# Summing k' over the tiles by accumulating DMAs, and another order of the part products

## The chip, the core and the metric

The kernel runs on one core of one Trainium2 chip. The metric is the time of one execution on the device in microseconds, as the median of a few runs. The profile is one execution of the same program, recorded by the hardware profiler.

## The reference

The inputs are x (2048 rows, D = 576 columns), a weight for q, k and v, an output weight, the two real DFT matrices over the sequence (2048 x 2048) and the two over D (576 x 576), and a gate vector. Cut to what matters:

```python
qkv = x @ wqkv                                  # q, k, v of 32 heads with 18 columns
phi = lambda t: where(t > 0, t + 1, exp(t)) + 1e-6
pq, pk = phi(q), phi(k)
kv  = einsum("bhsd,bhse->bhde", pk, v)
z   = einsum("bhsd->bhd", pk)                   # the sum of k' over the sequence
num = einsum("bhqd,bhde->bhqe", pq, kv)
den = einsum("bhqd,bhd->bhq", pq, z)[..., None] + 1e-6
a   = (num / den) @ wo
b   = dft_seq_re @ (x @ dft_hid_re.T) - dft_seq_im @ (x @ dft_hid_im.T)
g   = sigmoid((x * gate_w).sum(-1))
out = g * a + (1 - g) * b
```

## The kernel before

Every f32 product is made of three TensorE products of rounded parts: each operand is split into a high part (a ScalarE copy that rounds, `hi_of`, L167) and a low part (a VectorE subtraction, `lo_of`, L177), and high x high, high x low and low x high are added up in one PSUM bank. Nearly every matmul has 128 rows, 128 stationary columns and 288 moving columns, half of D.

The stages follow one another on TensorE:

- k' (L512 for the first four tiles of 128 rows of x, then L197): 16 tiles. `feature` makes k' from PSUM with two ScalarE operations and one VectorE operation (L336) and leaves it in `acc[i]`, an SBUF tile of 128 x 576 f32. `k_split` makes its two parts (`pk[i]`).
- k'^T x (L637): 20 steps, four for each of five column blocks c of x; a step takes four tiles. The x tiles `c` come by `xg_load` and are split by `xg_next` two steps ahead of their use. After the second step of each c, `kv_step` (L619, L622) multiplies by wv.
- In the same steps k' is summed over the 16 tiles for z. VectorE adds one `acc` tile to `zacc` in each step (`add`, L187). At step 15 `z_chain` adds the 16 epsilons (L585) and splits `zacc` into `zs`. At step 17 `z_sum` sums over the 128 partitions with four matmuls by a matrix of ones, and copies the two banks to `zb` (L593).
- q' (L197), the build of the matrix M and the product with it (L197), with transposes (L738) between.
- Twice, for the real and the imaginary part: the products over D (L903, in `product`), and the sequence products (L1058, in `sequence`). Both use seven products in place of eight (a Strassen-like scheme), with factors `fh` and `fl` (high and low) and sequence matrices `c`.

The matrix x for the products over D is prepared early: `Left(k, ...)` loads four quarters of a block of x (`xb<-in_xq_dram`, L352 and L358, by GpSimd's DMA queue), VectorE makes three combinations of them (L187), both engines split them, and GpSimd's queue stores them to DRAM (`xm<-xb`, L377). The blocks 2 to 6 go through two buffers in turn while k' and k'^T x run: the load of block k waits until the store of block k - 2 has left the buffer. Block 2 and block 4 use the same one. The weights for q' (`wqt`, L303) are later loaded into the same space, by the sync engine's queue, which also loads `xa` (L250) and `xg` (L538) in program order.

The order of ScalarE, VectorE and the sync engine's queue is written out by hand, in program order; GpSimd's and, up to the products over D, TensorE's order is set by a scheduler. Every engine works through its instructions in that order, and an instruction that waits holds all behind it.

The three parts of a product are taken in the order of

```python
FULL = ((0, 0), (0, 1), (1, 0))     # (part of the stationary, part of the moving operand)
```

in `product` (L903), `sequence` (L1058) and k'^T x (L637).

Of the kernel before, what the change touches and what calls it, by code (L numbers as in the profile page):

```python
# [8 lines left out]
F = mybir.dt.float32  # L9
R = mybir.dt.float32r  # L10
AF = mybir.ActivationFunctionType
ALU = mybir.AluOpType
AX = mybir.AxisListType

P = 128
S, D, H, DH = 2048, 576, 32, 18
NT = S // P
# [3 lines left out]
HALF = D // 2  # L21
FT = 4
CU = 4
NCU = NT // CU
NP = NT // 2
# [24 lines left out]
def gsize(g):  # L50
    return min(GW, D - g * GW)
# [15 lines left out]
XD = 2 * D * 4  # L67
T_AT = 0
ACC_AT = T_AT + NP * TPAIR
SLOT_AT, SLOT = ACC_AT + NT * D * 4 + 256, 7 * BS * P * 4  # L70
# [55 lines left out]
def kernel(  # L126
# [18 lines left out]
    nc = tc.nc  # L145
# [4 lines left out]
    def at(offset, shape, dtype=F, name="t"):  # L150
        count[0] += 1
        t = nc.alloc_sbuf_tensor_at(f"{name}_{count[0]}", list(shape), dtype,
                                    offset=base + offset)
        return t.ap()
# [8 lines left out]
    def bank():  # L163
        return psum.tile([P, 512], F, tag="bank", name="bank")
# [11 lines left out]
    def lo_of(dst, src, hi):  # L176
        nc.vector.tensor_tensor(out=dst, in0=src, in1=hi, op=ALU.subtract)  # L177
# [8 lines left out]
    def add(dst, a, b, op=ALU.add):  # L186
        nc.vector.tensor_tensor(out=dst, in0=a, in1=b, op=op)  # L187
# [11 lines left out]
    def half(h):  # L199
        return slice(h * HALF, (h + 1) * HALF)  # L200
# [35 lines left out]
    acc = [at(ACC_AT + i * D * 4, [P, D], F, "acc") for i in range(NT)]  # L236
# [10 lines left out]
    def load_next():  # L247
        if order:
            xs, raw = new_xs()
            nc.sync.dma_start(out=raw, in_=xa[order.pop(0)])  # L250
            raws.append((xs, raw))

    def split_next(lo_of=lo_of):
        if raws:
            xs, raw = raws.pop(0)
            hi_of(xs[:, 0:5], raw)
            lo_of(xs[:, 5:10], raw, xs[:, 0:5])
            split.append(xs)
# [126 lines left out]
    def left_part():  # L385
        while lefts:
            if next(lefts[0], True) is None:
                return
            lefts.pop(0)
# [44 lines left out]
    K_AT = T_AT + NT * XD  # L434
# [6 lines left out]
    def k_half(i, h, xs):  # L441
        ps = bank()[:, :HALF]
        run(ps, steps(xs, lambda j: wkt.row(h, j)))
        k_feature(i, h, ps)
# [39 lines left out]
    for h in range(2):  # L484
        ps = [bank()[:, :HALF] for _ in range(FT)]
        parts = wkt.split(h, KC)
        for c, (raw, hi, lo) in enumerate(first):
            passes = [(hi, c), (lo, c), (hi, 5 + c)][:3 if c < KC else 2]
            tiles = [range(FT)] * len(passes)
            if h == 0 and c == 0:  # L490
                a, b = ab
# [41 lines left out]
    def xg_load():  # L533
        if xg_order:
            c, q = xg_order.pop(0)
            o = cs_ring.next()
            raw = at(o + CU * P * 4, [P, CU, P], F, "craw")
            nc.sync.dma_start(out=raw, in_=xg[c, :, q * CU:(q + 1) * CU])  # L538
            xg_raw.append((c, at(o, [P, 2, CU, P], R, "c"), raw))

    def xg_next(lo_of=lo_of):
        if xg_raw:
            c, t, raw = xg_raw.pop(0)
            done.append(hi_of(t[:, 0], raw))
            if c == KC:
                lo_of(t[:, 0, :, REST:], raw[:, :, REST:], t[:, 0, :, REST:])
            else:
                lo_of(t[:, 1], raw, t[:, 0])
            xg_split.append(t)

    for i in range(FT, NT):
        xs = split.pop(0)
        k_half(i, 0, xs)
        if i < NT - 2:
            split_next()
        left_part()
        if i >= NT - 2:
            xg_next()
        held = pending[:]
        pending.clear()  # L560
        k_half(i, 1, xs)
        for f in held:
            f()
        if 8 <= i < 12:
            xg_load()
        if i < NT - 1:
            load_next()
        if i == FT:
            load_next()
        for k, j in ((3, 4), (4, 9), (5, 13)):  # L570
            if i == j:
                lefts.append(Left(k, SLOT_AT + 15104 + k % 2 * 14336, done[-1]).make())
# [2 lines left out]

    wqt = Wide(wq, LAY_Q, widths=QH)
    wq_splits = (s for h in (1, 0) for s in wqt.split(h, 2, lo_later))
    zacc = at(K_AT + 2 * XD, [P, D], F, "zacc")
    zs = at(K_AT + 3 * XD, [P, 2, D], R, "zs")
    zb = at(ZB_AT, [P, D], F, "zb")  # L580
    gt_ring, wv_ring = Ring(K_AT, XD, 2), Ring(WV_AT, XD, 2)
# [2 lines left out]
    def z_chain():  # L584
        nc.vector.tensor_scalar(zacc, zacc, NT * EPS, None, op0=ALU.add)  # L585
        hi_of(zs[:, 0], zacc)
        lo_of(zs[:, 1], zacc, zs[:, 0])

    def z_sum():
        for h in range(2):  # L590
            ps = bank()
            run(ps[:, :HALF], [(ones, zs[:, 0, half(h)]), (ones, zs[:, 1, half(h)])])
            nc.scalar.activation(zb[:, half(h)], ps[:, :HALF], AF.Copy)  # L593

    def load_pair(o, src, n=P):

# [9 lines left out]

    wvt, wot, gts = {}, [], {}
    FULL = ((0, 0), (0, 1), (1, 0))
    kv = [bank() for _ in range(3)]

    def kv_of(g):
# [12 lines left out]

    wvt[0], wv_split = load_pair(wv_ring.next(), wv[:, 0])
    wo_split = []
    step = 0
    for c in range(5):
        ps = [bank(), bank()]
        passes = FULL if c < KC else FULL[:2]  # L630
        for q in range(NCU):
            t = xg_split.pop(0)
            for k in range(CU):
                s = q * CU + k
                for n, (a, b) in enumerate(passes):
                    for h in range(2):
                        nc.tensor.matmul(ps[h][:, :HALF], t[:, a, k], pk[s][:, b, half(h)],  # L637
                                         start=(s == 0 and n == 0),
                                         stop=(s == NT - 1 and n == len(passes) - 1))
            tick()  # L640
            xg_load()
            if step == NT - 1:
                z_chain()
            xg_next(lo_later)
            if step in (1, 2):
                split_next(lo_later)
            if q == 1 and c:
                kv_step(c - 1)
            if q == 3 and c < 4 or step == 1:
                wv_split(lo_later)  # L650
            if q == 1 and c < 4:
                wvt[c + 1], wv_split = load_pair(wv_ring.next(), wv[:, c + 1])
            if step == 0:
                add(zacc, acc[0], acc[1])
            elif step < NT - 1:
                add(zacc, zacc, acc[step + 1])
            if step == NT + 1:
                z_sum()
            if step > NT:
                wo_split.pop(0)(lo_later)  # L660
            if NT - 1 <= step < NT + 4:
                g = step - NT + 1
                t, split_g = load_pair(wo_at[g], wo[g * GW:g * GW + gsize(g)], gsize(g))
                wot.append(t)
                wo_split.append(split_g)
            if q < NCU - 1:
                left_part()
            for k, j, o in ((6, 2, SLOT_AT + 15104), (NP, 6, ACC_AT)):
                if step == j:
                    lefts.append(Left(k, o, done[-1]).make())  # L670
            if step in (9, 12):
                wqt.load(step == 9)
            if step >= 13:
                next(wq_splits, None)
            step += 1
        gt = gts[c] = at(gt_ring.next(), [P, 2, D], R, "gt")
        for h in range(2):
            hi_of(gt[:, 0, half(h)], ps[h][:, :HALF])
            lo_later(gt[:, 1, half(h)], ps[h][:, :HALF], gt[:, 0, half(h)])
        left_part()  # L680
# [88 lines left out]
    def build_m(gs):  # L769
        for g in gs:  # L770
            n = gsize(g)
            for h in range(2):
                ps = bank()
                run(ps[:n, :HALF], [(kvb[:n, g, a, :n], wot[g][:n, b, half(h)])
                                    for a, b in FULL])
                nc.scalar.activation(mf[:n, g, half(h)], ps[:n, :HALF], AF.Copy)
# [86 lines left out]
    class Hidden:  # L863
# [33 lines left out]

        def product(self, ps, p, k, start):
            x, (w, wl) = self.x[p, k], self.w[k]
            ops = [(x[:, a, c * P:c * P + P], w[:, 2 * c + b]) for c in range(2) for a, b in FULL]  # L900
            ops.append((self.rest[p][:96, 6 - k], wl[:96]))
            for n, (a, b) in enumerate(ops):
                nc.tensor.matmul(ps, a, b, start=(start and n == 0), stop=(n == len(ops) - 1),  # L903
                                 skip_group_check=True)
# [112 lines left out]
    def sequence(m, g, src, dst, last=None, between=None):  # L1017
        late, held, stores, rest_lows = [], [], [], []
        for n in range(NP * NB):
            j, b = divmod(n, NB)  # L1020
            if b == 0:
                ps = {k: bank()[:, :HALF] for k in PRODUCTS}
# [3 lines left out]
            c = m.ready.pop(0)  # L1026
# [26 lines left out]
            for q, (l, f) in PRODUCTS.items():  # L1053
                for b, c in held:
                    for k in range(BS):
                        p = b * BS + k
                        for i, (x, y) in enumerate(FULL):
                            nc.tensor.matmul(ps[q], c[x][:, l, k], factors[p](y, f),  # L1058
                                             start=(p == 0 and i == 0),
                                             stop=(p == NP - 1 and i == 2))  # L1060
# [7 lines left out]
            y = at(Y_AT, [P, 2, 2, HALF], F, "ys")  # L1068
# [47 lines left out]
    for i in range(NT):  # L1116
# [3 lines left out]
        for h in range(2):  # L1120
            ps = bank()
# [164 lines left out]
```

## Time and profile before

| | |
|---|---|
| time, median of 3 runs | 733.61 us (733.57 to 733.9) |
| span of the profiled execution, first to last instruction | 730.4 us |
| median of the runs less that span | 3.2 us |
| TensorE busy | 724.2 us, 5444 matmuls |
| VectorE busy | 601.0 us |
| ScalarE busy | 335.6 us |
| GpSimd busy (its issues of DMAs included) | 57.0 us |
| granted TensorE clock | 1.000 |
| moved by DMA | 158.82 MB, 217 GB/s on average |

The profiler gives no time of its own for the profiled execution beside the span; what lies around the span is taken as the 3.2 us between it and the median. A matmul that follows another starts about 133 ns after it, though its record is 295 ns long, since matmuls are pipelined: the rate of a stretch is read from its length over its count. Times in the timeline and in the chain are microseconds from the span's start. In an answer of the timeline the bracket at the end of a row gives the idle time of the engine before it and who ended it.

### The profile page before, as it was taken

How to read it: one execution, taken by the hardware profiler on the slowest of the kernel's cores; microseconds unless marked ns; L12 is line 12 of the kernel's file. 1: busy time of each engine (PE TensorE's matmuls, PEld its weight loads, DVE VectorE, ACT ScalarE, POOL GpSimd, SP SyncE). 2: the span in 40 equal slices, each digit the busy share in tenths (PEclk: the TensorE clock that was granted, in tenths of full speed). 3: DMA queues.
4: the chain of work that ended last, by engine and by line, in shares of the span. 5: the costliest groups of instructions: out<-in, count | busy, mean ns of one | idle time of the engine just before them, and what ended most of it. 6: DMA issues, size and time to landing. Idle time of an engine off the chain costs nothing.

```text
span 730.4 us, 13876 instructions
## 1 busy us (share of the span) xinstructions
PE 724.2 (99%) x5444; PEld 722.4 (99%) x5444; DVE 601.0 (82%) x995; ACT 335.6 (46%) x522; POOL 57.0 (8%) x98
## 2 busy tenths in 40 slices
PE   8999999999999999999999999999999999999998
PEld 8999999999999999999999999999999999999997
DVE  5689866779999948989899989767889988788884
ACT  6898435678644444453344334323535332232231
POOL 1011200051032110000000000000000000000000
PEclk9999999999999999999999999999999999999999
DMA  7286787677477999644475666889964544544440
GB/s 254 84 275 217 265 296 234 226 215 224 155 221 298 362 312 383 211 153 135 165 240 177 228 233 202 296 279 395 374 219 130 171 145 135 156 149 148 152 152 33
DMA packets 54356, 158.82 MB, mean 217 GB/s; under 512 B 6420, under 2 KB 11092, under 8 KB 53268
## 3 DMA queue, kind: packets, MB, share of 16 engines
q1 hardware_dynamic: 45044, 118.90, 48.7%
q0 software_dynamic: 8960, 38.65, 14.6%
q8 instruction: 43, 0.70, 0.4%
q10 hardware_dynamic: 288, 0.39, 0.2%
q14 instruction: 21, 0.17, 0.1%
HBM read 115.05 MB, written 41.39 MB: 214 GB/s over the span
## 4 chain that ended last, share of the span: by engine, by line
PE 96%; DMA 2%; DVE 1%; ACT 0%; issue 0%; SPq 0%; DVEq 0%
PE bank L1058 48%; PE bank L197 23%; PE bank L903 14%; PE bank L637 7%; PE bank L512 2%; PE bank L738 1%; DMA wraw<-in_wk_dram 1%; DMA wf<-wm 1%; DMA craw<-in_xg_dram 1%; PE bank L619 0%; DVE row L1074 0%; ACT xb L167 0%; DVE ys L187 0%; PE bank L622 0%; ACT wd L167 0%
## 5 line engine op out<-in xcount | busy, mean ns | idle before, releaser
L1058 PE MATMUL bank<-fh,c 128*128 128x288 f32 x1792 | 357.5, 295 | 0.0
L1058 PEld LDWEIGHTS bank<-fh,c 128*128 128x128 f32 x1792 | 287.5, 188 | 0.0
L1058 PE MATMUL bank<-fl,c 128*128 128x288 f32 x896 | 264.2, 295 | 0.0
L167 ACT ACTIVATE c<-craw 128x1792 fp32r<-128x1792 f32 (+1 forms) x84 | 121.4, 1447 | 187.1 <-DVE craw L187 166.3
L1058 PEld LDWEIGHTS bank<-fl,c 128*128 128x128 f32 x896 | 168.9, 189 | 0.0
L177 DVE TENSOR_TENSOR c<-craw,c 128x1792 fp32r<-128x1792 f32 (+4 forms) x86 | 142.0, 1653 | 5.9 <-ACT c L167 5.7
L187 DVE TENSOR_TENSOR craw<-craw 128x256 f32<-128x256 f32 (+1 forms) x192 | 98.3, 512 | 25.2 <-DMA craw<-in_ci_dram 12.7
L197 PE MATMUL bank<-wd,xs 128*128 128x288 f32 (+1 forms) x784 | 106.3, 296 | 0.4 <-ACT wd L167 0.4
L197 PEld LDWEIGHTS bank<-wd,xs 128*128 128x128 f32 x784 | 104.7, 188 | 0.6 <-ACT wd L167 0.6
L903 PE MATMUL bank<-wf,xf 128*128 128x288 f32 x588 | 92.1, 297 | 0.2 <-DMA wf<-wm 0.2
L903 PEld LDWEIGHTS bank<-wf,xf 128*128 128x128 f32 x588 | 84.0, 189 | 0.4 <-issue 0.4
L197 PE MATMUL bank<-mw,qs 128*128 128x288 f32 x448 | 63.2, 297 | 0.0
L637 PE MATMUL bank<-pk,c 128*128 128x288 f32 x448 | 61.1, 296 | 0.1
L637 PEld LDWEIGHTS bank<-pk,c 128*128 128x128 f32 x448 | 59.9, 189 | 0.3 <-DVE c L177 0.3
L197 PEld LDWEIGHTS bank<-mw,qs 128*128 128x128 f32 x448 | 59.9, 188 | 0.2 <-DVE qs L177 0.2
L187 DVE TENSOR_TENSOR ys<-bank,ys 128x288 f32<-128x288 f32 x63 | 28.8, 457 | 16.1 <-PE bank L1058 12.4
L336 DVE SCALAR_TENSOR_TENSOR acc<-bank,e 128x288 f32<-128x288 f32 x64 | 28.3, 454 | 15.2 <-ACT e L335 13.7
L177 DVE TENSOR_TENSOR fl<-fl,fh 128x864 fp32r<-128x864 f32 (+1 forms) x32 | 34.6, 1093 | 7.1 <-ACT fh L167 5.8
L167 ACT ACTIVATE fh<-fl 128x864 fp32r<-128x864 f32 (+1 forms) x32 | 29.8, 950 | 16.2 <-DVE fl L187 16.2
L903 PE MATMUL bank<-wf,xr 96*128 96x288 f32 x112 | 33.3, 298 | 0.0
L1123 ACT ACTIVATE acc<-bank,gate 128x288 f32<-128x288 f32 x32 | 16.0, 500 | 35.1 <-PE bank L197 34.8
L187 DVE TENSOR_TENSOR ys<-ys,bank 128x288 f32<-128x288 f32 x47 | 21.2, 450 | 12.6 <-PE bank L1058 12.0
(107 smaller groups left out, 665.9 us busy)
## 6 DMA issues: line engine op xcount, KB each, us to landing
xf<-xm SPq DMA_DIRECT2D x42, 512.0 KB, 7.9
craw<-in_cr_dram SPq DMA_DIRECT2D x32, 512.0 KB, 4.1
craw<-in_ci_dram SPq DMA_DIRECT2D x32, 512.0 KB, 3.5
xraw<-in_xa_dram SPq DMA_DIRECT2D x28, 320.0 KB, 4.3
xm<-xb POOLq DMA_DIRECT2D x8, 1024.0 KB, 5.9
wf<-wm SPq DMA_DIRECT2D x14, 576.0 KB, 5.4
xr<-xr SPq DMA_DIRECT2D x14, 448.0 KB, 8.0
xm<-xb POOLq DMA_DIRECT2D x8, 768.0 KB, 5.9
```

The lines of the kernel that those rows point to most:

```text
L167: return nc.scalar.activation(dst, src, AF.Copy, bias=bias)
L177: nc.vector.tensor_tensor(out=dst, in0=src, in1=hi, op=ALU.subtract)
L187: nc.vector.tensor_tensor(out=dst, in0=a, in1=b, op=op)
L197: nc.tensor.matmul(ps, a, b, start=(n == 0), stop=(n == len(pairs) - 1))
L336: nc.vector.scalar_tensor_tensor(dst, ps, 0.0, e, op0=ALU.max, op1=ALU.add)
L512: nc.tensor.matmul(ps[i], x[:, i * P:(i + 1) * P], wkt.row(h, j), start=(c == 0 and n == (0 if h or i < 2 else 2)), stop=(c == KC and n == 1))
L637: nc.tensor.matmul(ps[h][:, :HALF], t[:, a, k], pk[s][:, b, half(h)], start=(s == 0 and n == 0), stop=(s == NT - 1 and n == len(passes) - 1))
L738: nc.tensor.transpose(banks[c // KC][:, (c % KC) * P:(c % KC + 1) * P], a, ident)
L903: nc.tensor.matmul(ps, a, b, start=(start and n == 0), stop=(n == len(ops) - 1), skip_group_check=True)
L1058: nc.tensor.matmul(ps[q], c[x][:, l, k], factors[p](y, f), start=(p == 0 and i == 0), stop=(p == NP - 1 and i == 2))
L1123: done.append(nc.scalar.activation(acc[i][:, half(h)], ps[:, :HALF], AF.Copy, scale=gate[:, i:i + 1]))
```

## The change

There are three parts.

1. `gather(i)` is a DMA on GpSimd's queue that adds `acc[i]` onto `acc[0]`, in SBUF. Fifteen of them take the place of the fifteen VectorE additions. The first three are placed after the first four tiles of k', and one follows each later tile. `acc[0]` is now `zacc`. Each gather waits for the one before it, as both write the same tile. `z_chain` moves from step 15 to step 10, `z_sum` from step 17 to step 11, and the copies to `zb` become `z_keep`, at step 12. The buffer of `Left(NP)` moves up by one tile, since `acc[0]` now stays in use.
2. The sequence products use the order `TURN = ((0, 1), (0, 0), (1, 0))`, but for the first batch of matrices, which stays with `FULL`.
3. The products over D use `TURN` as well.

The scheduler's order changes with it. On GpSimd's queue the gathers stand between the loads and stores of `Left`: gathers 1 to 3, the loads of block 3, gathers 4 to 6, first half of the store of block 2, gather 7, second half, gather 8, the loads of block 4, gather 9, first half of the store of block 3, gather 10, second half, gather 11, the loads of block 5, gather 12, first half of the store of block 4, gather 13, second half, gather 14, the loads of block 6, gather 15, and then the loads of the last block (`Left(NP)`). On TensorE the four matmuls of `z_sum` stand together after step 11, and twelve of the first products of q' stand together ahead of the last two steps of k'^T x, where before it was one.

```diff
+    zacc = acc[0]
+
+    def gather(i):
+        nc.gpsimd.dma_start(out=zacc, in_=acc[i], accum_op=ALU.add)
+
+    for i in range(1, FT):
+        gather(i)
     for i in range(FT, NT):
...
         for f in held:
             f()
+        gather(i)
...
-    zacc = at(K_AT + 2 * XD, [P, D], F, "zacc")
...
     def z_sum():
         for h in range(2):
             ps = bank()
             run(ps[:, :HALF], [(ones, zs[:, 0, half(h)]), (ones, zs[:, 1, half(h)])])
-            nc.scalar.activation(zb[:, half(h)], ps[:, :HALF], AF.Copy)
+            z_banks.append(ps)
+
+    def z_keep():
+        for h in range(2):
+            nc.scalar.activation(zb[:, half(h)], z_banks[h][:, :HALF], AF.Copy)
...
+    TURN = ((0, 1), (0, 0), (1, 0))
...
-    step = 0
+    step, Z = 0, 10
...
-            if step == NT - 1:
+            if step == Z:
                 z_chain()
...
-            if step == 0:
-                add(zacc, acc[0], acc[1])
-            elif step < NT - 1:
-                add(zacc, zacc, acc[step + 1])
-            if step == NT + 1:
+            if step == Z + 1:
                 z_sum()
+            if step == Z + 2:
+                z_keep()
...
-            for k, j, o in ((6, 2, SLOT_AT + 15104), (NP, 6, ACC_AT)):
+            for k, j, o in ((6, 2, SLOT_AT + 15104), (NP, 6, ACC_AT + D * 4)):
...
-            ops = [(x[:, a, c * P:c * P + P], w[:, 2 * c + b]) for c in range(2) for a, b in FULL]
+            ops = [(x[:, a, c * P:c * P + P], w[:, 2 * c + b]) for c in range(2) for a, b in TURN]
...
-                        for i, (x, y) in enumerate(FULL):
+                        for i, (x, y) in enumerate(TURN if n or b else FULL):
```

More of the change, by code (lines that the diff above doesn't have):

```diff
@@ L587, in z_chain @@
         lo_of(zs[:, 1], zacc, zs[:, 0])
+    z_banks = []
     def z_sum():
```

## The prediction

> **What bounds the kernel now.** I read the head of the page first, then the chain of work that ended last in order of time, then the windows by stage.
>
> ```profile
> span 730.4 us, 13876 instructions
> PE 724.2 (99%) x5444; PEld 722.4 (99%) x5444; DVE 601.0 (82%) x995; ACT 335.6 (46%) x522; POOL 57.0 (8%) x98
> ...
> 9.20 11.93 PE bank L512 x88
> 21.13 44.55 PE bank L197 x336
> 65.67 19.17 PE bank L637 x144
> ...
> 99.65 12.85 PE bank L637 x96
> ...
> 264.15 52.63 PE bank L903 x392
> 316.79 178.61 PE bank L1058 x1344
> ...
> 501.14 47.15 PE bank L903 x350
> 548.29 175.38 PE bank L1058 x1320
> ```
>
> TensorE is busy for 99% of the span, and the chain runs along it nearly from end to end. So only two things can change the time: another rate of its matmuls, or a wait of TensorE. The rate of a stretch is its length over its count: 44.55/336 = 132.6 ns in the products for k', (178.61 + 175.38)/2664 = 132.9 ns in the sequence products, (52.63 + 47.15)/742 = 134.5 ns in the products over D, 12.85/96 = 133.9 ns in k'^T x, and 11.93/88 = 135.6 ns in the first tiles of k', which include a few short halts.
>
> ```profile
> 66.00:117.00 51.00, 51.00 (x392) 51.00 (x391) 38.51 (x63) 23.03 (x39) 9.13 (x14) 1.00 0.75 249
> 117.00:127.00 10.00, 9.46 (x71) 9.13 (x71) 7.48 (x15) 6.93 (x14) 0.00 (x0) 1.00 0.90 266
> L187 DVE TENSOR_TENSOR zacc<-zacc,acc 128x576 f32<-128x576 f32 x14 | 10.5, 752 | 0.0
> ```
>
> The columns of the first two rows are the window, its length, and busy time with counts of TensorE, its weight loads, VectorE, ScalarE and GpSimd. In the stage where VectorE sums k' it is busy for 38.5 of 51 us and TensorE never stops. The additions that go, 15 by 752 ns = 11.3 us, lie wholly beside TensorE, so their removal is worth nothing by itself. The second window has the one halt that lies in this part of the kernel.
>
> **The sum of k' by gathers.** Nothing in the trace shows an accumulating DMA, so its time G, from issue to landing, has to be bounded.
>
> ```profile
> xm<-xb POOLq DMA_DIRECT2D x8, 1024.0 KB, 5.9
> xm<-xb POOLq DMA_DIRECT2D x8, 768.0 KB, 5.9
> att<-acc POOLq DMA_DIRECT2D x16, 288.0 KB, 5.3
> xb<-in_xq_dram POOLq DMA_DIRECT2D x16, 256.0 KB, 3.7
> ```
>
> These are sizes and median times to landing on the same queue. The nearest is the last one, which runs in the same stages: 3.7 us. From 256 to 1024 KB the time grows by 2.2 us, about 0.3 us for 100 KB, so 288 KB are 3.8 us. A gather also has to read the tile that it adds to; counted as another 288 KB this is 0.8 us, and G = 4.6 us. The low end is 3.8. The high end starts from 5.3 us, the row of the same size, whose transfers run in a busier stage, and is 6.1. I take 4.6.
>
> The Trainium skill's page "DMA: Bandwidth & Descriptors" (Anatomy of one DMA — SWDGE path) gives about 2.0 us and the bytes at 436 GB/s for such a transfer, an estimate of 2.7 us here; by it the gathers would have far more room. The row of 3.7 us for fewer bytes disagrees, and decides. The same page (Rules for kernel authors) speaks against summing this way: an accumulating DMA reads its destination and writes it later, so the next must wait for the completion of the one before. No run here shows that yet.
>
> The gathers therefore stand in line, 15 G in all. Who waits for them?
>
> ```profile
> 22.89 0.76 DVE L453 SCALAR_TENSOR_TENSOR pk<-acc,pk 128x576 fp32r<-128x576 f32 x1 [0.75 <-ACT pk L167]
> 23.67 0.46 DVE L336 SCALAR_TENSOR_TENSOR acc<-bank,e 128x288 f32<-128x288 f32 x1
> ...
> 61.70 0.75 DVE L187 TENSOR_TENSOR xb<-xb 128x256 f32<-128x256 f32 x2
> 62.37 0.69 DVE L177 TENSOR_TENSOR c<-craw,c 128x512 fp32r<-128x512 f32 x1
> ...
> 77.31 0.75 DVE L187 TENSOR_TENSOR xb<-xb 128x256 f32<-128x256 f32 x2
> ...
> 94.02 0.76 DVE L187 TENSOR_TENSOR xb<-xb 128x256 f32<-128x256 f32 x2
> ...
> 118.86 0.45 DVE L585 TENSOR_SCALAR zacc<-zacc 128x576 f32<-128x576 f32 x1
> ...
> 120.07 0.76 DVE L177 TENSOR_TENSOR zs<-zacc,zs 128x576 fp32r<-128x576 f32 x1 [0.75 <-ACT zs L167]
> 51.05 1.46 POOL L352 DMA_DIRECT2D xb<-in_xq_dram  x2 [6.36 <-ACT xs L167]
> 65.51 14.67 PE L637 MATMUL bank<-pk,c 128*128 128x288 f32 x109
> ```
>
> The first gather can go when the first tile has been read (22.89 + 0.76) and the second is whole (23.67 + 0.46): at 24.1 us. Two places wait.
>
> First, z. The four matmuls of `z_sum` now stand after step 11, that is 48 matmuls of 134 ns behind 99.65, at 106.1 us. From the start of `z_chain` to its last split the rows give 118.86 to 120.83, 2.0 us. So 24.1 + 15 G + 2.0 has to stay below 106.1, and G below 5.33. The split of the x tile for step 12 stands behind it on VectorE and has about the same limit.
>
> Second, block 4 of x. Before, its loads were issued at 51.05, ten microseconds ahead of its additions at 61.70. Now they stand behind gather 8 and wait for the second store of block 2, which stands behind gather 7, which waits for gather 6. That makes 24.1 + 6 G, 0.6 for the issue, 5.9 for the store, 0.7 for the issue of the first load, 3.7 for the second: 35.0 + 6 G. The additions (0.75) and the low part of the first x tile (0.69) stand behind on VectorE, so that part is there at 36.4 + 6 G. TensorE needs it for the fifth matmul of step 0, at 65.51 + 4 x 0.134 = 66.0. So G has to stay below 4.93. At 4.6 it is there at 64.0: 2 us to spare. Blocks 5 and 6 are reached in the same manner with more room, as their additions come at 77.31 and 94.02, about 16 us later each, and three gathers take 13.8.
>
> With G = 4.6 the last gather lands at 93.1 and costs nothing. Its cover is VectorE's lead over TensorE; with G above 4.93 that is gone, and every further 0.1 us costs 0.6, then 1.5 us.
>
> **z at steps 10 to 12.** This adds no work: four matmuls, three splits and two copies move. It could free the halt in the second window.
>
> ```profile
> 122.47 0.69 ACT L167 ACTIVATE gt<-bank 128x288 fp32r<-128x288 f32 x2
> 123.05 1.94 ACT L167 ACTIVATE xb<-xb 128x1024 fp32r<-128x1024 f32 x2
> 124.89 0.61 ACT L167 ACTIVATE c<-craw 128x512 fp32r<-128x512 f32 x1
> 125.41 0.67 ACT L167 ACTIVATE wd<-wraw 128x576 fp32r<-128x576 f32 x1
> 126.13 0.40 PE L197 MATMUL bank<-wd,xs 128*128 128x288 f32 x1 [0.44 <-ACT wd L167]
> 126.16 0.42 DVE L177 TENSOR_TENSOR c<-craw,c 128x256 fp32r<-128x256 f32 x1
> 126.50 0.75 DVE L177 TENSOR_TENSOR wd<-wraw,wd 128x576 fp32r<-128x576 f32 x1
> ```
>
> TensorE waits there for the weights of q' and an x tile, which stand on ScalarE behind `gt` and 1.9 us of work on a block of x. `gt` follows the end of a column block on TensorE, which doesn't move; so this queue starts no earlier. Moreover twelve products of q' now stand in front of the last two steps, and the second of them needs the low part of the weights, which came at 126.50 + 0.75 = 127.25. I let it come 0.4 us earlier, as z's work is gone from both engines ahead of it: 126.85, where before TensorE went on after c's low part, at 126.16 + 0.42 = 126.58. I count +0.2 us, rounded down from 0.27; the bounds are -1 (the halt goes) and +1 (another as long).
>
> **The order of the part products.** The same matmuls with the same operands run, in another order, with no further wait: all operands are there long before, and the first batch, where the low factors come late, stays as it was. `TURN` changes which operand neighbours share. In `FULL` the step from the second to the third part exchanges both operands; in `TURN` each step within a product exchanges one. The trace has no row with that order. What it has are rates of 132.6 to 135.6 ns for the same shape without waits that explain the differences, so what follows what seems to matter. If both stages reach the best row, 132.6: 0.3 ns x 2688 + 1.9 ns x 784 = 0.8 + 1.5 = 2.3 us less. If the sequence products go to 134.5 and those over D to 135.6: 1.6 x 2688 + 1.1 x 784 = 5.2 us more. I take the best row, since the order removes the only step that exchanges both operands; that is a choice. Against it speaks that in the first tiles of k' four neighbours share a moving operand and its rate is not better.
>
> **The sum.** 0 for the gathers, +0.2 for z, -2.3 for the order: -2.1 us. The span goes from 730.4 to 728.3, and the time from 733.6 to 731.5 with the same 3.2 us around it.
>
> **The rivals.**
>
> - *The gathers come too late* (slower). VectorE stops at the additions of block 4, or at `z_chain`, and TensorE behind it; it decides from G = 4.93. At 5.6 both places give +4.0 us (36.4 + 33.6 - 66.0, and 24.1 + 84 + 2.0 - 106.1); at 6.1 the second gives +11.5. With -2.1 from the rest: 735.5 and 743. For it: the accumulation is an unknown, and the queue then also carries the stores of x. Against: the nearest row leaves room. Chance 0.27.
> - *The order does nothing*, so the change as a whole does nothing: 733.8. For it: the first tiles of k'. Chance 0.18.
> - *The order costs*: +5.2 + 0.2, 739.0. For it: the sequence products stand already near the best row, so the room upward is larger. Chance 0.10.
>
> **How the numbers follow.** The forecast, 731.5, has the remaining 0.45. I call no change what lies within 0.2%, 1.5 us, which is about what a measurement of this kernel can tell. Faster is the forecast without its weaker part, but with rare larger gains of the order: 0.45. Within: 0.17. Slower: the rest of the first rival and the third: 0.38. The range has to hold the halt gone with the gain of the order (733.6 - 2.3 - 1 = 730.3) and something beyond the best row, so I begin it at 728.5; above it reaches to the high end of G, 743.
>
> **What would show it.** The gathers on GpSimd's queue: the distance between two of them is G, below 4.9 if I am right, and the last lands near 93 us. The additions of block 4 on VectorE should then not wait, and step 0 of k'^T x should start at 65.5 and run through. The four matmuls with ones should follow step 11 with no gap. The halt near 126 us should stay. The chain's stretches of sequence products and of products over D should give 132.6 ns a matmul. A gap of TensorE at 66 or at 106 us would prove the first rival, unchanged rates the second. It would be quite wrong if the products ran below 132 ns.

## The result, and the profile after

| | before | after |
|---|---|---|
| time, median of 6 runs each, same chip | 733.49 us (732.58 to 733.9) | 742.07 us (737.54 to 744.05) |
| ratio | | 1.0102, 95% interval 1.0076 to 1.0128 |
| span of the profiled execution | 730.4 us | 736.8 us |

The change makes the kernel slower by about 8.6 us. The prediction was 731.5 us, faster; the time lies inside its range, on the other side of no change. The profiled execution of after, at 738.49 us, is near the quick end of its six runs: the two shortest have a mean granted clock of 0.994, the other four, of 742 to 744 us, 0.990 to 0.991.

The head of the page after, then the chain of waits (start, length, what), cut to the stretches that answer to those of before:

```profile
span 736.8 us, 13892 instructions
PE 723.6 (98%) x5444; PEld 721.2 (98%) x5444; DVE 591.4 (80%) x980; ACT 336.1 (46%) x522; POOL 70.5 (10%) x113
...
275.73 49.41 PE bank L915 x371
325.14 177.15 PE bank L1070 x1344
...
508.24 46.67 PE bank L915 x350
```

The sequence products take 177.15/1344 = 131.8 ns a matmul, where it was 132.9, and those over D 46.67/350 = 133.3 ns in the second pass, where it was 134.7. So this part of the change gained. But the first stretch over D, which began at 264.15, now begins at 275.73 (its piece is cut 21 matmuls later, which is 2.8 us of that): about 8.8 us were lost before it. The windows of k'^T x say where (window, length, busy time and count of TensorE, its weight loads, VectorE, ScalarE and GpSimd, granted clock, DMA share, GB/s):

```profile
66.00:77.00 11.00, 6.27 (x29) 6.04 (x28) 6.51 (x13) 4.16 (x7) 2.67 (x4) 0.69 0.86 265
77.00:117.00 40.00, 40.00 (x307) 40.00 (x306) 23.89 (x39) 17.00 (x29) 12.26 (x17) 1.00 0.95 290
117.00:130.00 13.00, 13.00 (x101) 12.89 (x100) 4.91 (x10) 3.92 (x8) 0.53 (x1) 1.00 0.83 271
```

In the first window TensorE starts 29 matmuls where the distance of 134 ns would give 82. It is without work for nearly 5 us, and its granted clock is 0.69. After 77 us nothing is lost for 40 us. The timelines of TensorE and of VectorE in that window show one wait, on both:

```profile
65.61 0.68 PE L651 MATMUL bank<-pk,c 128*128 128x288 f32 x4
71.01 9.27 PE L651 MATMUL bank<-pk,c 128*128 128x288 f32 x49 [4.73 <-DVE c L177]
...
69.60 0.76 DVE L187 TENSOR_TENSOR xb<-xb 128x256 f32<-128x256 f32 x2 [7.72 <-DMA xb<-in_xq_dram]
70.28 0.68 DVE L177 TENSOR_TENSOR c<-craw,c 128x512 fp32r<-128x512 f32 x1
```

TensorE stops after exactly four matmuls of step 0. It waits for the low part of an x tile (L177), which stands on VectorE behind the additions of block 4 (L187), and these wait for the loads of block 4. This is the place, and the wait, of the first rival. GpSimd's timeline shows how the loads came to be late:

```profile
24.53 0.95 POOL L554 DMA_DIRECT2D acc<-acc  x1 [11.65 <-DVE acc L336]
29.38 0.89 POOL L554 DMA_DIRECT2D acc<-acc  x1 [3.90 <-DVE xb L187]
...
54.72 0.86 POOL L554 DMA_DIRECT2D acc<-acc  x1 [3.34 <-DMA acc<-acc]
55.35 0.78 POOL L377 DMA_DIRECT2D xm<-xb  x1
60.31 0.84 POOL L554 DMA_DIRECT2D acc<-acc  x1 [4.18 <-DVE xs L177]
62.42 1.50 POOL L352 DMA_DIRECT2D xb<-in_xq_dram  x2 [1.26 <-ACT c L167]
...
98.17 0.91 POOL L554 DMA_DIRECT2D acc<-acc  x1 [0.61 <-DMA acc<-acc]
```

The engine that a bracket names is often not the true releaser here: the gather has to wait for the one before it. Gather 7 goes at 54.72, (54.72 - 24.53)/6 = 5.03 us after another. Behind it stands the second store of block 2 (55.35), whose buffer the loads of block 4 need: they go at 62.42, where before it was 51.05.

The DMA view of after (size, median us from issue to landing), of the gathers and of their neighbours on the queue:

```profile
xm<-xb POOLq DMA_DIRECT2D x8, 1024.0 KB, 6.8
xm<-xb POOLq DMA_DIRECT2D x8, 768.0 KB, 6.3
acc<-acc POOLq DMA_DIRECT2D x15, 288.0 KB, 4.7
xb<-in_xq_dram POOLq DMA_DIRECT2D x16, 256.0 KB, 4.3
```

A gather takes 4.7 us, and the others 0.4 to 0.9 us more than before. The loads of block 4 themselves, issued in the window of 62 to 64.5 us, took a median of 5.7, where before those of block 4 took 4.1:

```profile
xb<-in_xq_dram POOLq DMA_DIRECT2D x2, 256.0 KB, 5.7
```

### The profile page after: what moved, and what is told of

The parts are those of the page before. It is cut to its first block, busy times and chain, and to the rows that moved or that the text cites. A ratio compares the mean times of both kernels' runs of the same rounds, so it can differ in the third digit from the quotient of the medians.

```text
span 736.8 us, 13892 instructions
## 1 busy us (share of the span) xinstructions
PE 723.6 (98%) x5444; PEld 721.2 (98%) x5444; DVE 591.4 (80%) x980; ACT 336.1 (46%) x522; POOL 70.5 (10%) x113
## 2 busy tenths in 40 slices
DMA packets 56517, 163.25 MB, mean 222 GB/s; under 512 B 6660, under 2 KB 11332, under 8 KB 55428
## 4 chain that ended last, share of the span: by engine, by line
PE 77%; DMA 3%; DVE 2%; ACT 1%; issue 0%; SPq 0%; DVEq 0%; ACTq 0%
PE bank L1070 45%; PE bank L197 16%; PE bank L915 14%; PE bank L750 1%; DMA craw<-in_ci_dram 1%; DMA xm<-xb 1%; DMA craw<-in_xg_dram 1%; PE bank L651 1%; DVE fl L177 1%; DVE c L177 1%; DMA wf<-wm 1%; ACT xb L167 1%; DVE craw L187 0%; DVE row L1086 0%; ACT c L167 0%
## 5 line engine op out<-in xcount | busy, mean ns | idle before, releaser
L177 DVE TENSOR_TENSOR c<-craw,c 128x1792 fp32r<-128x1792 f32 (+4 forms) x86 | 141.9, 1653 | 18.6 <-ACT c L167 18.4
L187 DVE TENSOR_TENSOR craw<-craw 128x256 f32<-128x256 f32 (+1 forms) x192 | 98.3, 512 | 24.2 <-DMA craw<-in_ci_dram 12.7
L651 PE MATMUL bank<-pk,c 128*128 128x288 f32 x448 | 63.8, 304 | 5.5 <-DVE c L177 5.5
L651 PEld LDWEIGHTS bank<-pk,c 128*128 128x128 f32 x448 | 62.4, 196 | 5.9 <-DVE c L177 5.9
L187 DVE TENSOR_TENSOR ys<-bank,ys 128x288 f32<-128x288 f32 x63 | 28.8, 457 | 15.8 <-PE bank L1070 12.6
L177 DVE TENSOR_TENSOR fl<-fl,fh 128x864 fp32r<-128x864 f32 (+1 forms) x32 | 34.6, 1093 | 6.7 <-ACT fh L167 5.5
L187 DVE TENSOR_TENSOR ys<-ys,bank 128x288 f32<-128x288 f32 x47 | 21.1, 449 | 12.1 <-PE bank L1070 11.6
```

## The experiments

Each ran beside the kernel before on the same chip, whose median was 733.3 to 733.7 us each time. Theory A, formed from the trace: the gathers stand in line and hold up the loads behind them; the halt near 66 us and the lower clock after it are the loss, and the order of the part products is a gain. The rivals were that the gathers' traffic delays everything (C), that the order or the earlier z costs, and others given with each run.

**The order alone.** The kernel before with

```diff
-            ops = [... for c in range(2) for a, b in FULL]
+            ops = [... for c in range(2) for a, b in TURN]
-                        for i, (x, y) in enumerate(FULL):
+                        for i, (x, y) in enumerate(TURN if n or b else FULL):
```

> The kernel before with the order TURN in the products over D and in the sequence products, and nothing else. Theory A (the loss comes from the gathers, the order gains): in the trace of the changed kernel the first sequence products ran at 177.15/1344 = 131.8 ns against 132.9 before, so about 1.5 us less in each sequence stage and 0.3 us less in each stage of products over D, and 0.9 us more at a halt in the second sequence stage: 731 us, ratio 0.996 to 0.998. Rival B (the order does nothing or costs): 733 to 739 us, ratio 1.000 or above.

Measured: 729.32 us, ratio 0.9939 (0.9918 to 0.9960). The chain of waits:

```profile
263.77 51.98 PE bank L904 x392
315.75 177.16 PE bank L1059 x1344
...
498.82 46.71 PE bank L904 x350
545.53 173.99 PE bank L1059 x1320
```

Against the stretches of the same counts before, the sequence products gain 1.45 + 1.39 = 2.8 us, and those over D 0.65 + 0.44 = 1.1 us. So the order gains about 4 us, more than theory A said, and the rest of the change costs about 13 (742.07 against 729.32).

**The gathers alone.** The changed kernel with `FULL` at both places.

> The changed kernel with FULL everywhere: the gathers and the early z alone. Theory A (late gathers hold the loads of block 4 of x, VectorE stands at its additions, TensorE at step 0 of k'^T x): a halt of TensorE near 66 us of 4 to 8 us, then a stretch at a lower granted clock, and 744 us, ratio 1.014 (1.010 to 1.018). Rival B (the order causes part of the loss): 738 us or below.

Measured: 746.18 us, ratio 1.0169 (1.0133 to 1.0205). The windows:

```profile
66.00:77.00 11.00, 5.91 (x30) 5.91 (x31) 6.52 (x13) 3.77 (x6) 3.53 (x5) 0.69 0.86 241
117.00:130.00 13.00, 9.47 (x56) 9.36 (x55) 4.83 (x10) 4.16 (x8) 0.00 (x0) 0.74 0.87 287
```

The halt near 66 is there, now of 5.4 us, and a second one of 3.7 us begins at 120.8, also with a lower clock behind it. There TensorE waits for an x tile whose load stands on SP's queue behind the load of wq, which was held until 115.7 by late stores of x. The two parts of the change nearly add up: 12.5 and -4.3 against the 8.6 of the whole.

**The lower clock taken away.** The changed kernel with 36 matmuls that nobody reads put in just ahead of the fifth matmul of step 0, so that TensorE is busy for most of the wait:

```diff
+                    if step == 0 and k == 0 and n == 2:
+                        filled = bank()
+                        for _ in range(36):
+                            nc.tensor.matmul(filled[:, :HALF], t[:, 0, k], pk[s][:, 0, half(0)],
+                                             start=True, stop=True)
```

> The changed kernel with 36 extra matmuls of the usual shape (4.8 us) on TensorE ahead of the fifth matmul of step 0, into a bank that nobody reads: TensorE works where it stood still for 4.9 us. Theory A1 (the 240 ns a matmul after the halt are a lower granted clock that the halt itself brings on): the matmuls after it start 132 to 134 ns apart, the granted clock of the window 66 to 77 us is near 1.00 and not 0.69, the low part of the x tile comes as late as before, and the time falls by about 2.5 us: 739.5 where the changed kernel has 742, ratio 1.007 to the kernel before. Rival A2 (they are slow for another reason, as the crowd of DMAs): 240 ns stays and the time does not fall; with the extra work it rises if the halt is shorter than 4.8 us.

Measured: 742.99 us, ratio 1.0120 (1.0083 to 1.0157). The same windows:

```profile
66.00:77.00 11.00, 9.69 (x73) 9.46 (x73) 6.38 (x13) 2.90 (x5) 3.62 (x6) 1.00 0.79 210
117.00:130.00 13.00, 8.99 (x58) 8.71 (x57) 4.54 (x10) 4.28 (x9) 0.00 (x0) 0.87 0.87 302
```

The halt that is left is 1.6 us and the clock is 1.00: with TensorE busy the clock isn't lowered. But the time did not fall to the 739.5 us that theory A1 gave. In this trace TensorE stops for 4.2 us at 121, which it does not do in the trace of after. The run with the gathers alone has a halt there too, beside the whole first one. In both runs the loads of block 4 go at 65.2 to 65.3 us, against 62.42 in the trace of after, though their edits lie behind that place. So the filled wait need not have brought on the second halt; whether filling it gains anything stays open.

**Two chains.** Even tiles onto `acc[0]`, odd ones onto `acc[1]`, so that a gather waits only for the last but one; VectorE adds the two sums in `z_chain`:

```diff
-        nc.gpsimd.dma_start(out=zacc, in_=acc[i], accum_op=ALU.add)
+        nc.gpsimd.dma_start(out=acc[i % 2], in_=acc[i], accum_op=ALU.add)
...
-        nc.vector.tensor_scalar(zacc, zacc, NT * EPS, None, op0=ALU.add)
+        nc.vector.scalar_tensor_tensor(zacc, zacc, NT * EPS, acc[1], op0=ALU.add, op1=ALU.add)
```

> The changed kernel with the gathers in two chains, even tiles onto tile 0 and odd tiles onto tile 1, joined by VectorE in the instruction that adds the epsilons: the same 288 KB and the same place in the queue for each gather, but each waits for the last but one. Theory A (it is the waiting in line that makes the stores and loads of x late): the store of block 2 and the loads of block 4 go out 10 us earlier, no halt at 66 us, and 731 to 732 us, ratio 0.997 to 0.999. Rival C (it is the traffic of the gathers on the DMA engines that makes everything later): the halt stays, 738 us or more.

Measured: 734.45 us, ratio 1.0008 (0.9983 to 1.0033). The DMA view and two windows:

```profile
xm<-xb POOLq DMA_DIRECT2D x8, 1024.0 KB, 7.6
...
acc<-acc POOLq DMA_DIRECT2D x14, 288.0 KB, 6.2
...
66.00:77.00 11.00, 11.00 (x85) 11.00 (x84) 7.74 (x13) 7.00 (x12) 1.21 (x3) 1.00 1.02 289
...
84.50:88.00 3.50, 3.34 (x19) 3.34 (x20) 3.47 (x8) 1.13 (x2) 0.00 (x0) 0.73 1.03 407
```

The time lies between the two forecasts. The loads of block 4 now go at 54.3 and the halt near 66 is gone, and with it 7.6 us of the loss. So A holds for the largest part. The rest, 5 us over the order alone, speaks for C. With two gathers in flight each of them takes longer, 6.2 us, and so do the stores of x. A halt of 2.6 us at 82, again with a lower clock behind it, comes from the loads of block 5. These wait for the second store of block 3, which is issued 3.3 us later than before (64.32 against 61.05) and takes 11.6 us where it took 4.9.

**Plain copies.** The changed kernel with the gathers at the same places, but without the addition:

```diff
-        nc.gpsimd.dma_start(out=zacc, in_=acc[i], accum_op=ALU.add)
+        nc.gpsimd.dma_start(out=zacc, in_=acc[i])
```

> The changed kernel, but each gather is a plain copy of its tile onto the first one, at the same place in GpSimd's line and still one behind the other (so the sum over tiles is left out, and the output is not the reference's). Theory A1: the accumulation itself, which reads its target too, makes the gathers long. Then a copy lands in about 3.8 us, the gathers start 4.4 us apart instead of 5.0 in the first six, the seventh is issued at about 51, the loads of block 4 at 55 to 58, and the halt near 66 is gone or under 1 us; the time is about 733. Rival A2: what counts is the line, that is landing, signal and the next issue one after the other, whatever the transfer does. Then the spacing stays at 4.8 to 5.2 us, the halt near 66 at 4 us or more, and the time at 738 to 742.

Measured: 729.49 us in one run. GpSimd's timeline, the DMA view of the window of 24 to 45 us, and that of the whole run:

```profile
24.63 0.58 POOL L554 DMA_DIRECT2D acc<-acc  x1 [11.66 <-DVE acc L336]
...
45.06 0.55 POOL L554 DMA_DIRECT2D acc<-acc  x1 [1.99 <-DVE acc L336]
...
55.01 1.44 POOL L352 DMA_DIRECT2D xb<-in_xq_dram  x2 [3.58 <-ACT e L335]
...
acc<-acc POOLq DMA_DIRECT2D x6, 288.0 KB, 2.5
...
xm<-xb POOLq DMA_DIRECT2D x8, 1024.0 KB, 6.5
xm<-xb POOLq DMA_DIRECT2D x8, 768.0 KB, 6.8
acc<-acc POOLq DMA_DIRECT2D x15, 288.0 KB, 4.3
xb<-in_xq_dram POOLq DMA_DIRECT2D x16, 256.0 KB, 4.3
```

The first six copies land after 2.5 us, where the first six gathers took 4.5, so there the addition costs about 2 us of each. Over all fifteen the difference is small, 4.3 against 4.7: beside the stores of x a plain copy takes about as long. But it is the first six that stand ahead of block 4. The seventh goes at 45.06 instead of 54.72, block 4 at 55.01 instead of 62.42, and the whole loss is gone: 729.5 is the time of the order alone. A1 holds, and the copies were even quicker than it said. The profile counts as many bytes as for the changed kernel, 163.25 MB, and the stores and loads of x are about as slow as there (6.5, 6.8 and 4.3 us). So this slowness alone costs nothing; it is the length of the gathers ahead of block 4, in a line, that does.

**The sum on VectorE, z early.** The changed kernel without gathers; two additions in each of the first eight steps of k'^T x:

```diff
-        gather(i)
...
+            if step < 8:
+                for i in range(2 * step + 1, min(2 * step + 3, NT)):
+                    add(zacc, zacc, acc[i])
```

> The changed kernel without its gathers: VectorE adds two tiles of k' onto the first one in each of the first eight steps of k'^T x, and z is still made from step 10 on, with the turned order kept. Theory A (the whole loss comes from the accumulating DMAs and what they delay): no halt near 66, the clock stays at 1.00 in 66 to 77, and the time is that of the turned order alone, 729.3, within 1 us. Rival B (z earlier, or the left part's other place, costs by itself): a halt over 1 us between 77 and 125, and the time is 731 or more. The halt near 126, which ends with a piece of x, stays in both.

Measured: 728.56 us, ratio 0.9927 (0.9906 to 0.9948).

```profile
66.00:77.00 11.00, 11.00 (x85) 11.00 (x84) 10.82 (x17) 8.44 (x14) 2.03 (x3) 1.00 0.62 215
117.00:130.00 13.00, 13.00 (x101) 12.97 (x100) 8.30 (x14) 8.47 (x15) 0.00 (x0) 1.00 0.83 265
```

No halt near 66, so the earlier z and the new place of the last block cost nothing. The halt near 126, which I expected to stay, is gone as well: TensorE is busy for all 13 us of the second window. This is the lowest median of all, but its interval overlaps with that of the order alone, so whether the earlier z gains anything stays open.

**Loads of blocks 4 and 5 from ScalarE's queue.**

```diff
-                    begin_after(nc.gpsimd.dma_start(...), after)
+                    q = nc.scalar if k in (4, 5) else nc.gpsimd
+                    begin_after(q.dma_start(...), after)
```

> The changed kernel, its gathers and order kept; only the loads of blocks 4 and 5 of x (L352) are issued from ScalarE's queue instead of GpSimd's, so that they stand behind no gather. Theory A (the loss comes from loads that stand behind waiting gathers in GpSimd's line): the loads of block 4 are issued at 51 to 53, the halt near 66 and the lower clock behind it are gone, and the time is 729 to 731.5. Rival C (the gathers' own traffic makes the loads and stores late wherever they are issued): the halt near 66 may go, but others near 88 and 121 come in its place, 3 us or more in all, and the time is 733 to 738.

Measured: 755.81 us, ratio 1.0311 (1.0288 to 1.0333), a miss for both theories. GpSimd's and ScalarE's timelines:

```profile
57.94 0.78 POOL L378 DMA_DIRECT2D xm<-xb  x1
...
63.01 1.03 ACTq L353 DMA_DIRECT2D xb<-in_xq_dram  x2
64.09 0.41 ACT L334 ACTIVATE e<-bank 128x288 f32<-128x288 f32 x1 [19.19 <-issue]
```

The load did not go at 51 to 53. It waits for the second store of block 2, which went at 57.94 behind its gather, and ScalarE waited with it for 19 us, and TensorE for 15, and for 7 more at 83. So what the gathers hold up first is the store, as the prediction's sum had it, and not the load; I had drawn up this run by a shorter version of the theory. A load that waits belongs on a queue where nothing else stands behind it.

**Other orders.** Two runs on the kernel before, to see what in the order gains.

```diff
+    REV, CROSS = ((1, 0), (0, 0), (0, 1)), ((0, 1), (1, 0), (0, 0))
...
+                   for a, b in (CROSS if self.lay.swap else REV)]
...
+    enumerate(FULL if n < NB else CROSS if last is None else REV):
```

> The kernel before with other orders of the part products. Products over D: low-high, high-high, high-low in the first pass (each neighbour shares one operand with the next), high-low, low-high, high-high in the second (only the last two share). Sequence products: the second of these orders in the first stage, the first of them in the second stage. Theory O1 (the gain comes from sharing an operand at both steps): about 132.6 ns a matmul over D in the first pass and 134.7 in the second; 132.9 in the first sequence stage and 131.8 in the second; the time lies about 2 us under the kernel before. Rival O2 (the gain comes from starting with high-low): 134.3 and 133.5 over D, 131.8 and 132.9 in the sequences, and about the same time. Rival O3 (the order is nothing, the gain is from elsewhere): 134.3 and 134.7, 132.9 and 132.9, no change.

Measured: 731.34 us, ratio 0.9973 (0.9950 to 0.9995). The chain:

```profile
267.30 49.74 PE bank L905 x371
317.04 177.48 PE bank L1060 x1344
500.39 46.66 PE bank L905 x350
547.05 174.49 PE bank L1060 x1320
```

That is 132.1 and 132.2 ns in the two sequence stages, one with each order (`CROSS`, `REV`), though the first 168 matmuls of each stay with `FULL`. In 80 us behind those, 345 to 425 and 575 to 655, there are 609 matmuls with `CROSS` and 608 with `REV`, against 609 with `TURN` and 604 or 605 with `FULL`. Over D it is 133.3 ns with `CROSS` in the second pass, about as with `TURN`. In the first pass `REV` gains little: 49.74 us for these 371 matmuls, against 49.97 with `FULL` (the gathers alone) and 49.41 with `TURN` (after). All three accounts fall: both orders gain in the sequences, and `CROSS`, which shares an operand at a single step, as much as `TURN`. What both have, `TURN` as well, and `FULL` has not, is two neighbours with the same moving operand. The next run tests that:

```diff
+    PAIR, SWAP = ((1, 0), (0, 1), (0, 0)), ((0, 0), (1, 0), (0, 1))
...
+                   for a, b in (PAIR if self.lay.swap else SWAP)]
...
+    enumerate(FULL if n < NB else PAIR if last is None else SWAP):
```

> The kernel before with two more orders. One is low-high, high-low, high-high, in which no matmul has the moving operand of the one ahead of it; it is used in the first sequence stage and in the second pass over D. The other is high-high, low-high, high-low, in which the second keeps the moving operand of the first; it is used in the second sequence stage and in the first pass over D. Theory O4 (the gain comes from keeping the moving operand): 132.9 ns a matmul in the first sequence stage as with the old order and 132.1 or less in the second; over D 132.6 to 133.3 in the first pass and 134.5 or more in the second; about 731. Rival O5 (the old order alone is slow, because it starts with high-high): 132.1 and 132.9 in the sequences. Rival O6 (any order but the old one gains): 132.1 in both.

Measured: 731.62 us, ratio 0.9976 (0.9960 to 0.9992).

```profile
265.06 52.33 PE bank L905 x392
317.38 178.59 PE bank L1060 x1344
495.97 52.55 PE bank L905 x392
548.52 174.69 PE bank L1060 x1320
```

The order without a kept moving operand gives 132.9 ns in the first sequence stage, the same as `FULL`; the one with it gives 132.3 in the second. Over D it is 133.5 with it, in the first pass, where `FULL` had 134.3, and 134.1 without, in the second. This is as O4 has it in direction, with smaller distances than it gave; O5 and O6 fall.

One stretch fits no account. The first 168 matmuls of the second sequence stage stay with `FULL` in both runs, as in the kernel before. They take 22.35 us before and in this run, but 22.13 us in the run with `REV` and `CROSS`, which is 1.3 ns less for each, about the rate of `TURN`. So a kept moving operand goes with the gain in these stages as wholes, but the rate depends on something else besides, which no run here isolates.

**The turned order elsewhere.** The order alone, and `steps` turned too, which serves k', q' and the last product:

```diff
-            yield xs[:, c], rhs(c)
-            yield xs[:, c], rhs(5 + c)
-            yield xs[:, 5 + c], rhs(c)
+            pairs = ((c, c), (c, 5 + c), (5 + c, c))
+            for j, k in pairs if whole else (pairs[1], pairs[0], pairs[2]):
+                yield xs[:, j], rhs(k)
```

> The turned order alone, as in the run of that name, and beside it the turned order in the products for k' (from the second tile on), for q' and in the last product, 1232 more matmuls. If an operand shared at both steps gains there what it gains in the sequences, 1.1 ns a matmul, these stages go from 132.6 to about 131.5 ns and the time is 1.4 us under that of the turned order alone, near 728. If these stages have another limit (they stand at 132.5 with the old order, not 132.9), the time stays at 729.3.

Measured: 730.35 us, ratio 0.9957 (0.9936 to 0.9979), no better than the order alone. In the chain the two long stretches of these products read

```profile
21.18 44.63 PE bank L197 x336
138.31 47.69 PE bank L197 x356
```

and that is 132.8 and 134.0 ns, against 132.6 and 133.3 with the old order. So keeping the moving operand gains nothing there, and why the order gains in the sequences stays open.

## Why the prediction was wrong

*The spacing of the gathers: the step that failed.* The prediction bounded G, the time of one gather from issue to landing, and took 4.6 us. The size came out right: the median is 4.7, 4.5 for the first six. But that was luck: its two terms were 3.8 for moving the tile and 0.8 for reading the target, and the first six copies show 2.5, which leaves 2.0 for the addition. (The formula that the prediction cited from the Trainium skill's page "DMA: Bandwidth & Descriptors", Anatomy of one DMA, gives 2.7; these copies agree with it, at 2.5, and the additions do not.) The mistake was to set the line at 15 G. That the next gather has to wait for the one before it was foreseen, and the same page of the Trainium skill (Rules for kernel authors) asks for that wait; what it costs beyond the landing was left out. In the trace the next of the first seven gathers starts 0.6 to 0.8 us after the one before has landed (the first goes at 24.53 and lands after 4.2, and the next goes at 29.38). So the distance is 5.03 us in the first six and (98.17 - 24.53)/14 = 5.26 over all. The limit that the prediction had worked out, 4.93, is passed. In the traces of the gathers alone and of the filled wait the first six distances are 5.4 and 5.5.

*The neighbours' transfers.* The prediction priced the second load of block 4 at 3.7 us, from a row of before; here it took 6.3. It asked which transfers stand behind the gathers, but not what becomes of the times of these transfers. By its own sum the additions of block 4 could begin at 35.0 + 6 x 4.6 = 62.6; they began at 69.60. Of these 7.0 us, 0.4 come from the first gather, 2.6 from the spacing, 0.4 from the store, 0.9 from the issue of the loads, 2.6 from the load, and the remaining 0.1 from the way to VectorE. The sum had 2.0 us to spare. The first gather and the spacing use up 3.0 by themselves, which would have made a halt of 1 us; the other 4.0 make up the rest of the halt. What made the load slow is not shown: with the gathers alone the same loads, issued 2.8 us later, took 3.7.

*The lower clock: a step that was missing.* The prediction priced a late part at its lateness. The halt itself is 4.9 us longer than a plain step, and the first 23 matmuls after it start 240 ns apart instead of 134, 2.4 us more. The clock in the window is 0.69, and in the run with the filled wait 1.00. Halts of 0.9 to 1.6 us left it at 1.00, one of 2.6 us gave 0.73 behind it, one of 3.7 us 0.74 in its window. The Trainium skill's page "TensorE: Matmul & The Clock Gate" (Part 1: The HAM clock gate) says that the array falls to half its clock after an idle window of about 3.4 us, and comes back after about as long of work. The trace agrees that a halt brings it on: the granted clock is 1.00 from 66 to 69.7 us and 0.50 from 69.8 to 76.6. But the slow stretch behind the halt lasts 23 x 240 ns = 5.5 us, and a halt of 2.6 us was enough for one.

*z.* The place at 106 us, the prediction's other limit, did not bind: TensorE came there 7.4 us later, at 113.52, and the last gather had landed by 98.17 + 4.4 = 102.6. The halt near 126 stayed, as said, and stands at 134 as 0.8 us, with another of 0.9 at 129.8 from a late piece of x. With the sums on VectorE and z early it goes, so the lower bound given, -1, can be reached. The earlier z alone did not do it: with the plain copies a halt of 0.7 us is still there at 126.

*The order.* Right in sign, and mis-sized: -2.3 predicted, about -4 measured. Over D 1.5 was predicted and 1.1 found; in the sequences 0.8 and 2.8. The prediction stopped at the best rate that any row of before had, 132.6 ns, and `TURN` goes below it, to 131.8; below 132 was the prediction's own sign of being quite wrong. Its reason, that each step exchanges only one operand, is not what the runs show: `CROSS`, which exchanges both at one step, gains as much in the sequences. What the reason is stays open.

*The sum.* Against the order alone the profiled execution of after has a span longer by 736.8 - 726.3 = 10.5 us. The halt near 66 is 4.9 of it, the slow matmuls 2.4, the halt at 129.8 is 0.9, and one at 571.7, where a low factor comes late, 0.8. Of the remaining 1.5, 0.4 lie ahead of 21 us, where the long stretch of k' begins at 21.2 instead of 20.8, and 0.4 are a halt at 275.2; the rest I could not put down to one place. The median of after is 3.6 us longer still than its profiled execution. A second halt, as the gathers alone have it at 121, would explain that: their trace has two stretches of lower clock and a mean granted clock of 0.991, like the longer runs of after. But no trace of such an execution of after was taken.

## What to carry to other kernels

A DMA that has to wait for the one before it costs its landing and the way to the next issue, and everything on its queue waits with it: set up the line in distances, with the transfers that stand between, and ask what the new traffic does to their own times. A late part that stops TensorE for some microseconds can also cost the clock behind it (here 2.4 us on top of 4.9), so a small miss is dearer than it looks. Work that an engine does beside the bottleneck is free already: here VectorE's additions, made earlier but left on VectorE, did as well as the order alone or better, and only the order is shown to gain.

## What the hardware showed unexpectedly

- A DMA of 288 KB within SBUF, one at a time and with little beside it, took 2.5 us as a copy and 4.5 as an addition onto its target. Over all fifteen, most of them beside the stores of x, it was 4.3 and 4.7; with two chains of additions in flight, 6.2.
- The order of three matmuls with the same operands changes their rate by 0.8%. In 80 us of a sequence stage there are 604 or 605 matmuls in `FULL`, 605 in the other order that keeps no moving operand, 607 or 608 where the first two share it, and 609 where the last two do, `TURN` among them. In the products for k', q' and the last product it gains nothing, and 168 matmuls in `FULL` ran once at the rate of `TURN`.
- A halt of TensorE of 2.6 us was enough for a lower clock behind it.
